# Second FFN weights kept split in DRAM, double buffers for the spectral evictions, and Winograd input sums in five steps

## The chip, the cores and the metric

The kernel runs on one core of a Trainium2 chip. The core has a matrix engine (TensorE, PE in the profile; its weight loads are listed as PEld), a vector engine (VectorE, DVE), a scalar engine (ScalarE, ACT), GpSimd (POOL) and SyncE (SP), which here only issues DMAs. Each engine works through its own queue of instructions in order and waits on semaphores that other engines or DMAs raise. Matmul operands come from SBUF, an on-chip memory of 128 partitions, and results go to PSUM banks, which VectorE and ScalarE read. DRAM is reached by DMA alone.

The metric is the device time of one execution in microseconds. The kernel before takes 1140.56 us, the median of three runs.

## The reference

The reference adds three things for a prompt `u` of 2048 rows by 576 channels: `u` itself, a state-space convolution (S4) and a feed-forward network, the last two on the layer-normalised rows.

```python
dt = exp(log_dt); A = A_re + 1j*A_im; B = B_re + 1j*B_im; C = C_re + 1j*C_im
P = exp((dt*A)[:, :, None] * l[None, None, :])          # 576 x 128 x 2048
K = einsum("dn,dnl,dn->dl", C, P, dt*B).real            # the kernel of the convolution
y = irfft2(rfft2(pad(xn.T)) * rfft2(pad(K)))[:, :2048].T + xn * Dskip
h = silu(xn @ w1)                                       # 576 -> 4608
out = u + y + h @ w2                                    # 4608 -> 576
```

All is float32.

## The kernel before, in words

**Precision.** TensorE's float32 products are made from two parts: a value `x` is split into `xh`, a rounded copy made by ScalarE, and `xl = x - xh`, made by VectorE. A product is the sum of three matmuls, `wh*xh + wh*xl + wl*xh`. So every weight tile costs a cast on ScalarE and a subtraction on VectorE before TensorE can use it.

**The FFN** sets the order of the work. Rows are processed in two halves of 1024 rows, each half in two blocks (b) of 512; the 4608 hidden channels in nine chunks (c) of four tiles (t) of 128. `up` (L278) makes one hidden tile for 512 rows: matmuls into `ph`, the SiLU and the split into `gh`, `gl` (L294 to L296). `down` (L298) multiplies four hidden tiles with the second weights for 128 rows, into two PSUM tiles `po` of 288 columns (L309), and VectorE adds each to the output accumulator `acc` (L313). The weights come with `load_w1` (L235) and `load_w2` (L260, a 288 KB DMA on SP's queue, L264) into the raw tiles `w1r` and `w2r`; `split_w1` and `split_w2` (L267) make the parts: ScalarE casts `w2h` (L273), VectorE subtracts `w2l` (L275).

**Second half, from its chunk 2 on.** `wino_ffn` (L421) takes over for seven chunks, as 14 units n of two hidden tiles. It computes the `up` matmuls of both blocks together by a Winograd form of a 2x2 block product: seven products instead of eight. `prod` (L438) is one product of six matmuls of 512 columns, `rest` (L444) adds the last 64 channels, `gate` (L447) is the SiLU and split. `prep` prepares sums of weights (L362 to L369) and their splits (`split`, L355 and L356) for the next unit. The seven products go to four accumulators: `pb`, `ps_a`, `ps_c` and the SBUF tile `f5`; the `down` steps `d[0]` to `d[3]` of the unit before lie between them. The second weights of a unit are loaded and split there by `second` as in the other chunks. The sums of the inputs S1, S2, S3, S4 are made once by `wino_x` (L548): VectorE joins the parts (L554), forms sums, and splits them again (L559, L560).

**The convolution** is worked in as side work between the FFN's steps: `side` yields at fractions of the FFN's 276 steps, and each piece is put into the program when the FFN has come that far. The tables and the kernel K are made in the first half (`kgen`). `wino_x` runs whole at 0.6215. `spectral` (L852) runs from there to 0.855, in 32 steps k: it loads two tables `m2`, `m3` on POOL's queue (L855), loads and splits a 128-row tile of both spectra on SP's queue (`load_split`), multiplies them into `pk` and `pu` (L943), forms the complex product in `ka`, `kb` (L870 to L879: ScalarE evicts `pk`, VectorE multiplies by `pu`), splits it into `yh`, `yl`, multiplies back into `pb`, and stores 288 KB `yo` to the DRAM tensor `d2` (L894, POOL). Each step is written one ahead: `front(k+1)` comes before the back part of k.

**The tail.** From 0.895 on, `tail` loads the results: `conv_load` (L946) reads a conv tile `ys` from `d2` in two DMAs (L950), with six buffers; `load_r0` (L905) reads back the first half's sums `r0` (576 KB for two row tiles). In the second half's last chunk, and for the first half's rows in `last` (L907), `add_conv` (L953) multiplies `ys` with a table (L964), and VectorE adds the result (L971); then the rows are stored. Conv tiles 8 to 15 belong to the second half, 0 to 7 to the first. The tail's loads are written behind `pins["load"]`, the last weight load issued; such a pin orders an instruction behind another on the same engine's queue.

**Who sets the order.** The program's order gives priorities; a scheduler then orders each engine's queue by when it estimates operands ready, so a queue can differ from the source's order. Blocks marked high priority (evictions, gates, `acc` adds) go ahead of other ready work.

**Buffers.** Pools give each tag a number of rotating buffers, and a tile's first write waits for the last reader of the tile that had the buffer. `w2h` and `w2l` have five each, `w2r` two, `ka` and `kb` one, all from pools that are named in the code.

Of the kernel before, what the change touches and what calls it, by code (L numbers as in the profile page):

```python
# [17 lines left out]
P = 128  # L18
# [23 lines left out]
def kernel(  # L42
# [185 lines left out]
    def ffn():  # L228
# [31 lines left out]
        def load_w2(half, c, t):  # L260

            first = half == 0 and c == 0
            r2 = (pa if first and t > 1 else wp).tile([P, D], F32, tag="w2r", name="w2r", bufs=2)
            pins["load"] = nc.sync.dma_start(r2, w2v[:, c * FT + t, :]).ins  # L264
            R2[half, c, t] = r2

        def split_w2(half, c, t):  # L267
            first = half == 0 and c == 0
            r2 = R2.pop((half, c, t))
            h2 = wp.tile([P, D], F32R, tag="w2h", name="w2h", bufs=FT + 1)  # L270
            l2 = wp.tile([P, D], F32R, tag="w2l", name="w2l", bufs=FT + 1)
            with behind(pins["xt_s"] if first else pins["gh"]):
                pins["w2h"] = nc.scalar.copy(h2, r2).ins  # L273
            with behind(pins["w1l"] if first else None):
                nc.vector.tensor_sub(l2, r2, h2)  # L275
            W2[half, c, t] = h2, l2

# [20 lines left out]
        def down(blk, jj, terms=None):  # L298
# [4 lines left out]
            for h in range(2):  # L303
                hs = slice(h * HD, (h + 1) * HD)
                po = ps2.tile([P, 512], F32, tag="ps2", name="po")
                n = 0
                for gs, ws in terms:
                    for g, w in ((0, 0), (0, 1), (1, 0)):
                        pins["pe"] = nc.tensor.matmul(po[:, :HD], gs[g][:, js], ws[w][:, hs],  # L309
                                                      start=n == 0, stop=n == 3 * len(terms) - 1).ins  # L310
                        n += 1
                with tc.high_priority():
                    nc.vector.tensor_add(acc[j][:, hs], po[:, :HD], acc[j][:, hs])  # L313
# [74 lines left out]
        for i, blk in enumerate(plain[:-1]):  # L388
# [15 lines left out]
            for step in ("u0", "d0", "d1", "d2", "d3", "u1", "u2", "u3"):  # L404
# [14 lines left out]
        yield from wino_ffn(load_w1, load_w2, split_w2, prep, WT, first, end, W2, plain[-1], down)  # L419

    def wino_ffn(load_w1, load_w2, split_w2, prep, WT, first, end, W2, before, down):  # L421

# [63 lines left out]
        for n in range(first, end):  # L486
            d = downs(n - 1)
            pb = ps2.tile([P, 512], F32, tag="ps2", name="pb2")
            f5 = wino["pool"].tile([P, 512], F32, tag="f5", name="f5", bufs=1)
            prod(pb, unit("c1", n, 0), A[0], start=True)  # L490
            with tc.high_priority():
                nc.scalar.copy(ps_a, pb)
            prod(ps_c, unit("t13", n, 0), S1, start=True)
            rest(ps_c, "c2", n, 2, x41)
            with tc.high_priority():
                nc.scalar.copy(f5, ps_c)
            yield 0
            d[0]()
            second(n, 0, "split")
            second(n + 1, 0, "load")  # L500
            yield 0
            prod(pb, unit("t24", n, 0), S2)
            with tc.high_priority():
                nc.vector.tensor_add(ps_c, pb, f5)
            d[1]()
            prep(n + 1, "c2")
            yield 0
            prod(pb, unit("t13", n, 2), S3)
            with tc.high_priority():
                nc.vector.tensor_add(f5, pb, f5)  # L510
            d[2]()
            prep(n + 1, "c1")
            prep(n + 1, "sums")
            yield 0
            d[3]()
            second(n, 1, "split")
            second(n + 1, 1, "load")
            yield 0

            def lower():  # L520
                gate(f5, 1, 2 * n + 1)
                prod(pb, unit("t24", n, 2), A22)
                gate(pb, 1, 2 * n)

            def upper():
                prod(ps_c, unit("c2", n, 0), S4)
                rest(ps_c, "c2", n, 2, d4)
                gate(ps_c, 0, 2 * n + 1)
                prod(ps_a, unit("c1", n, 2), A[1])
                rest(ps_a, "c1", n, 4, x40)  # L530
                gate(ps_a, 0, 2 * n)

            rest(pb, "c1", n, 4, x41, stop=False)
            for k, f in enumerate((lower, upper) if n % 2 == 0 else (upper, lower)):
                f()
                prep(n + 1, ("t13", "t24")[k])
                yield 0
# [10 lines left out]
    def wino_x(sx, xp):  # L548

        (ah, al, x40), (bh, bl, x41) = xts[2], xts[3]  # L550

# [11 lines left out]
        def new(name):  # L563
# [4 lines left out]
        d4 = xp.tile([P, 512], F32R, name="d4")  # L568
        x21, x22 = join(bh, bl, 0, "x21"), join(bh, bl, 2, "x22")
        nc.vector.tensor_add(x22, x21, x22)  # L570
# [13 lines left out]
        yield 0  # L584
        S3 = parts(x21, bh[:, 0:2], bl[:, 0:2])
        wino["x"] = ([(ah[:, 0:2], al[:, 0:2]), (ah[:, 2:4], al[:, 2:4])], (bh[:, 2:4], bl[:, 2:4]),
                     S1, S2, S3, S4, x40, x41, d4)
        wino["pool"] = xp

    kl = yp = pa = tail_at = None  # L590
    kf = {}
# [260 lines left out]
    def spectral():  # L852
# [5 lines left out]
        def front(k):  # L858
# [118 lines left out]
    def side():  # L977
        nonlocal s4, kl, yp, pa, tail_at
        marks = (0.1357, 0.613, 0.855)
# [136 lines left out]
```

## Time and profile before

| what | value |
|---|---|
| three runs | 1140.56, 1141.24, 1139.49 us; median 1140.56 |
| the profiled execution | 1145.05 us, its span 1143.3 us, mean granted clock 0.995 |
| TensorE busy | 1101.7 us, 96% of the span |
| VectorE busy | 981.5 us, 86% |
| ScalarE busy | 735.9 us, 64% |
| GpSimd busy | 98.5 us, 9% |
| moved by DMA | 151.26 MB, 132 GB/s on average |
| w2 casts on ScalarE (L273) | 72, 47.7 us |
| w2 subtractions on VectorE (L275) | 72, 53.5 us |
| input sums of the Winograd form | joins begin at 665.10 us |
| spectral stage | tables loaded from 685.5 us, last matmul ends at 1066.45 us |

A row of costly groups reads: line, engine, operation, output tile, its operands, shapes and count, then busy time in us and mean ns of one, then the idle time of that engine just before these instructions and what ended most of it. A row of waits reads: engine, waiting line, what ended the wait, the total in us, how often, the longest. A row of stretches gives, between two times, the busy time and count of each engine, the granted TensorE clock as a share of full speed, the mean busy share of the 16 DMA engines and the GB/s moved. A row of DMA issues gives the queue, the count, the KB of each and the median us from issue to landing. A row of the chain gives the start, the length and what ran on the path that ended last. In a timeline row the bracket is the idle time before the instruction and what released it. Matmuls overlap in the array, so the durations of single matmuls are longer than the distance between two starts.

### The profile page before, as it was taken

The page shows a single profiled execution, that of the slowest core. Times are in us where ns is not written, and L with a number is a line of the kernel's source. Part 1 is how long each engine was busy: PE and PEld are TensorE (multiplying, and loading weights), DVE is VectorE, ACT ScalarE, POOL GpSimd, SP SyncE. Part 2 cuts the span into 40 slices and gives each one's busy share as a digit, 9 for nine tenths or more (in the row PEclk, how much of TensorE's full clock was granted, in tenths as well). Part 3 has the DMA queues.
Part 4 walks back from the last instruction along what each step waited for, and adds up shares of the span by engine and source line. Part 5 has one row for each costly group of instructions (what it writes and reads, how often), then busy time and mean ns, then how long its engine had stood idle before and what let it go on. Part 6 is the DMA issues. An engine that isn't in the chain of part 4 may idle for free.

```text
span 1143.3 us, 23137 instructions
## 1 busy us (share of the span) xinstructions
PE 1101.7 (96%) x9101; PEld 989.3 (87%) x9101; DVE 981.5 (86%) x1675; ACT 735.9 (64%) x1297; POOL 98.5 (9%) x178
## 2 busy tenths in 40 slices
PE   6999999999999999999999989999999999999878
PEld 5998998988889898898899977999899888999766
DVE  6698999999999999999999688998898779888535
ACT  4665557676667677667676437787878667877310
POOL 1001000000000000000000001111111111110012
PEclk9999999999999999999999999999999999999989
DMA  9456412424232525175924136445444445442697
GB/s 272 132 161 214 126 35 80 103 91 102 90 92 60 138 74 127 47 202 187 244 75 109 44 74 181 133 138 152 135 113 144 136 133 151 149 144 90 148 236 229
DMA packets 167372, 151.26 MB, mean 132 GB/s; under 512 B 87984, under 2 KB 136128, under 8 KB 166624
## 3 DMA queue, kind: packets, MB, share of 16 engines
q1 hardware_dynamic: 150128, 112.66, 35.8%
q0 software_dynamic: 16752, 36.24, 10.1%
q8 instruction: 72, 1.18, 0.4%
q10 hardware_dynamic: 384, 0.89, 0.3%
q14 instruction: 36, 0.29, 0.1%
HBM read 103.74 MB, written 46.08 MB: 131 GB/s over the span
## 4 chain that ended last, share of the span: by engine, by line
PE 59%; DVE 18%; DMA 9%; ACT 9%; issue 3%; SPq 1%; DVEq 0%; ACTq 0%
PE po L309 26%; PE ph L286 14%; PE pb L438 3%; DMA w1r<-in_B_w_dram 3%; PE kp L818 2%; DVE acc L313 2%; PE pc L438 2%; PE z L833 1%; PE ph L287 1%; PE ph L288 1%; PE pk L943 1%; DMA dxt<-xt 1%; PE pu L943 1%; DVE w1l L356 1%; PE pb L943 1%
## 5 line engine op out<-in xcount | busy, mean ns | idle before, releaser
L309 PE MATMUL po<-w2h,gh 128*128 128x288 f32 x1152 | 339.7, 299 | 7.5 <-DVE acc L313 5.4
L309 PE MATMUL po<-w2l,gh 128*128 128x288 f32 x1152 | 339.1, 297 | 0.4 <-DVE w2l L275 0.4
L309 PE MATMUL po<-w2h,gl 128*128 128x288 f32 x1152 | 336.1, 297 | 0.6 <-DVE gl L296 0.6
L309 PEld LDWEIGHTS po<-w2h,gh 128*128 128x128 f32 x1152 | 216.1, 189 | 21.8 <-DVE acc L313 8.4
L309 PEld LDWEIGHTS po<-w2l,gh 128*128 128x128 f32 x1152 | 216.9, 189 | 8.1 <-issue 2.3
L309 PEld LDWEIGHTS po<-w2h,gl 128*128 128x128 f32 x1152 | 215.5, 189 | 3.3 <-DVE gl L296 0.9
L313 DVE TENSOR_TENSOR acc<-po,acc 128x288 f32<-128x288 f32 x296 | 129.0, 450 | 29.0 <-PE po L309 27.5
L286 PE MATMUL ph<-xh,w1h 128*128 128x512 f32 (+1 forms) x368 | 99.4, 387 | 0.9 <-ACT xh L123 0.6
L286 PE MATMUL ph<-xl,w1h 128*128 128x512 f32 (+1 forms) x368 | 98.6, 383 | 0.0
L286 PE MATMUL ph<-xh,w1l 128*128 128x512 f32 (+1 forms) x368 | 97.3, 382 | 0.0
L294 ACT ACTIVATE gf<-ph 128x512 f32<-128x512 f32 (+1 forms) x92 | 52.9, 576 | 44.3 <-PE ph L288 26.8
L273 ACT CAST w2h<-w2r 128x576 fp32r<-128x576 f32 x72 | 47.7, 674 | 47.8 <-PE po L309 32.6
L286 PEld LDWEIGHTS ph<-xl,w1h 128*128 128x128 f32 x368 | 66.5, 189 | 12.4
L286 PEld LDWEIGHTS ph<-xh,w1l 128*128 128x128 f32 x368 | 66.6, 188 | 12.1
L286 PEld LDWEIGHTS ph<-xh,w1h 128*128 128x128 f32 x368 | 65.3, 191 | 11.0 <-ACT xh L123 0.9
L777 ACT ACTIVATE c<-th,magic 128x1040 f32<-128x1040 f32 x36 | 42.0, 1167 | 43.8 <-DVE C L798 34.1
L296 DVE TENSOR_TENSOR gl<-gf,gh 128x512 fp32r<-128x512 f32 (+1 forms) x92 | 60.5, 659 | 8.8 <-ACT gh L295 8.4
L779 ACT ACTIVATE c<-th 128x1040 f32<-128x1040 f32 x36 | 38.7, 1074 | 37.9 <-DVE th L778 37.8
L295 ACT CAST gh<-gf 128x512 fp32r<-128x512 f32 (+1 forms) x92 | 55.3, 602 | 7.7 <-PE po L309 6.4
L855 POOL DMA_DIRECT2D m<-in_cm_dram x64 | 34.5, 540 | 295.8 <-PE pu L943 196.1
L157 POOL DMA_DIRECT2D d1u<-u x32 | 17.4, 542 | 451.6 <-ACT u L156 451.6
L275 DVE TENSOR_TENSOR w2l<-w2r,w2h 128x576 fp32r<-128x576 f32 x72 | 53.5, 749 | 2.0 <-ACT w2h L273 1.8
(268 smaller groups left out, 2449.6 us busy)
## 6 DMA issues: line engine op xcount, KB each, us to landing
w2r<-in_B_w_dram SPq DMA_DIRECT2D x72, 288.0 KB, 3.9
w1r<-in_B_w_dram SPq DMA_DIRECT2D x35, 512.0 KB, 3.8
d1u<-u POOLq DMA_DIRECT2D x32, 288.0 KB, 2.7
d1k<-stage SPq DMA_DIRECT2D x18, 512.0 KB, 7.2
ur<-d1u SPq DMA_DIRECT2D x32, 288.0 KB, 3.0
kr<-d1k SPq DMA_DIRECT2D x32, 288.0 KB, 2.8
d<-yo POOLq DMA_DIRECT2D x32, 288.0 KB, 2.8
ys<-d SPq DMA_DIRECT2D x32, 288.0 KB, 9.6
```

What stands on the lines that cost most here:

```text
L273: pins["w2h"] = nc.scalar.copy(h2, r2).ins
L275: nc.vector.tensor_sub(l2, r2, h2)
L286: nc.tensor.matmul(ph, w[:, kt, :], v[:, kt, a:e], start=n + kt == 0, stop=False)
L294: nc.scalar.activation(gf, ph, AF.Silu)
L295: pins["gh"] = nc.scalar.copy(gh, gf).ins
L296: pins["gl"] = nc.vector.tensor_sub(gl, gf, gh).ins
L309: pins["pe"] = nc.tensor.matmul(po[:, :HD], gs[g][:, js], ws[w][:, hs], start=n == 0, stop=n == 3 * len(terms) - 1).ins
L313: nc.vector.tensor_add(acc[j][:, hs], po[:, :HD], acc[j][:, hs])
L438: pins["pe"] = nc.tensor.matmul(dst, a[:, kt], v[:, kt], start=start and n == 0, stop=stop and n == 5, skip_group_check=True).ins
L777: nc.scalar.activation(c65, th, AF.Identity, bias=magic)
L779: nc.scalar.activation(c65, th, AF.Abs)
L855: nc.gpsimd.dma_start(m, cm23[:, k, i:i + 2])
```

## The change

It has four parts.

First, a DRAM tensor `dw2` is added, with room for the split second weights of seven chunks (28 tiles of 128 partitions by 2 by 576). In the first half, `split_w2` of the chunks 2 to 8 stores the parts there after splitting, one DMA of 576 KB a tile on SP's queue. In the second half, `second` no longer loads and splits these weights; it reads the parts back with one DMA of 576 KB a tile on POOL's queue, straight into the tile that the matmuls use. `w2h` and `w2l` become the two halves of one tile `w2`. The raw `w2r` buffers move to another pool, which exists in the first part of the kernel as well.

Second, `ka` and `kb` get two buffers each, and the split of `ka` into `yh`, `yl` is written ahead of `front(k+1)`, where it was written at the end of `front(k)`.

Third, `wino_x` yields five times, at steps 171 to 175 of 276, and its parts are spread over them: joins; S1; S2; S3 and the sum for S4; S4 and the small `d4`. The spectral stage starts at step 176 (before 0.6215 of 276, which is step 171.5), and its end mark stays at 0.855.

Fourth, the two inputs of the Winograd form change places (`xts[3], xts[2]`), and the products of a unit become named functions. The first unit has an order of its own: p1, d0, c11 and d1, d2, then p5, p6 and d3, then p7, and at the end c12 and c2x. In the later units the products keep their order; only the accumulators' roles are named anew.

```diff
+    dw2 = dram.tile([NFT - WINO_C * FT, P, 2, D], F32, name="dw2")
...
         def load_w2(half, c, t):
-            r2 = (pa if first and t > 1 else wp).tile([P, D], F32, tag="w2r", name="w2r", bufs=2)
+            r2 = (pa if first else kfp).tile([P, D], F32, tag="w2r", name="w2r", bufs=4 if first else 2)
             pins["load"] = nc.sync.dma_start(r2, w2v[:, c * FT + t, :]).ins
...
         def split_w2(half, c, t):
-            h2 = wp.tile([P, D], F32R, tag="w2h", name="w2h", bufs=FT + 1)
-            l2 = wp.tile([P, D], F32R, tag="w2l", name="w2l", bufs=FT + 1)
+            W2[half, c, t] = w = wp.tile([P, 2, D], F32R, tag="w2", name="w2", bufs=FT + 1)
+            h2, l2 = w[:, 0], w[:, 1]
...
-            W2[half, c, t] = h2, l2
+            if half == 0 and c >= WINO_C:
+                nc.sync.dma_start(dw2[(c - WINO_C) * FT + t], w.bitcast(F32))
...
-        def second(n, i, part):
-            if first <= n < end:
+        def second(n, i):
+            if n < end:
                 f = 2 * n + i
-                (load_w2 if part == "load" else split_w2)(1, f // FT, f % FT)
+                w = wp.tile([P, 2, D], F32R, tag="w2", name="w2", bufs=FT + 1)
+                pins["load"] = nc.gpsimd.dma_start(w, dw2[f - WINO_C * FT]).ins
+                W2[1, f // FT, f % FT] = w
...
-        for i in range(2):
-            second(first, i, "load")
+        second(first, 0)
...
+            def c11():
+                prod(ps_a, units["c1", n, 2], A[1])
+                rest(ps_a, "c1", n, 4, x40)
+                gate(ps_a, 1, 2 * n)
+            def c12():
+                prod(ps_c, units["c2", n, 0], S4)
+                rest(ps_c, "c2", n, 2, d4)
+                gate(ps_c, 1, 2 * n + 1)
+            def c2x():
+                gate(f5, 0, 2 * n + 1)
+                prod(pb, units["t24", n, 2], A22)
+                gate(pb, 0, 2 * n)
+            def c1x():
+                c12()
+                c11()
+            def side_w(k):
+                if k == 1:
+                    prep(n + 1, "c2")
+                elif k == 2:
+                    prep(n + 1, "c1")
+                    prep(n + 1, "sums")
+                elif k == 3:
+                    second(n, 1)
+                    second(n + 1, 0)
+            if n == first:
+                order = ((p1, 0), (c11, 1), (2,), (p5, p6, 3), (p7,))
+                ends = c12, c2x
+            else:
+                order = ((p1, p5), (0,), (p6, 1), (p7, 2), (3,))
+                ends = (c1x, c2x) if n % 2 == 0 else (c2x, c1x)
...
     def wino_x(sx, xp):
-        (ah, al, x40), (bh, bl, x41) = xts[2], xts[3]
+        (ah, al, x40), (bh, bl, x41) = xts[3], xts[2]
...
         x21, x22 = join(bh, bl, 0, "x21"), join(bh, bl, 2, "x22")
+        S1, S2, S4 = new("s1"), new("s2"), new("s4")
+        S3 = bh[:, 0:2], bl[:, 0:2]
...
+        yield 0
         nc.vector.tensor_add(x22, x21, x22)
-        S1 = parts(x22, *new("s1"))
+        parts(x22, *S1)
+        yield 0
         x11 = join(ah, al, 0, "x11")
         nc.vector.tensor_sub(x21, x11, x21)
         nc.vector.tensor_sub(x11, x22, x11)
-        S2 = parts(x11, *new("s2"))
+        parts(x11, *S2)
+        yield 0
+        parts(x21, *S3)
         x12 = join(ah, al, 2, "x12")
         nc.vector.tensor_sub(x12, x12, x11)
-        S4 = parts(x12, *new("s4"))
+        yield 0
+        parts(x12, *S4)
...
-        S3 = parts(x21, bh[:, 0:2], bl[:, 0:2])
...
-            ka = kl.tile([P, D], F32, tag="ka", name="ka")
-            kb = kl.tile([P, D], F32, tag="kb", name="kb")
+            ka = kl.tile([P, D], F32, tag="ka", name="ka", bufs=2)
+            kb = kl.tile([P, D], F32, tag="kb", name="kb", bufs=2)
...
-            return m3, split_of(ka, "y", 1)
+            return m3, ka
...
-            m3, ys = nxt
+            m3, y = nxt
+            ys = split_of(y, "y", 1)
             if k < 31:
                 nxt = front(k + 1)
...
-            for _ in wino_x(sx, xp):
-                yield 0.6215
+            for k, _ in enumerate(wino_x(sx, xp)):
+                yield (171 + k) / 276
         with tc.tile_pool(name="kl", bufs=1) as kl:
             for at in spectral():
-                yield 0.6215 + (at - 1) * (marks[2] - 0.6215)
+                yield 176 / 276 + (at - 1) * (marks[2] - 176 / 276)
```

More of the change, by code (lines that the diff above doesn't have):

```diff
@@ L418, in ffn, with wino_ffn @@
                         prep(first, early[step])
-        yield from wino_ffn(load_w1, load_w2, split_w2, prep, WT, first, end, W2, plain[-1], down)
-    def wino_ffn(load_w1, load_w2, split_w2, prep, WT, first, end, W2, before, down):
+        yield from wino_ffn(load_w1, prep, WT, first, end, W2, plain[-1], down)
+    def wino_ffn(load_w1, prep, WT, first, end, W2, before, down):
         ps_a = ps1.tile([P, 512], F32, tag="ps1", name="pa")
@@ L489, in wino_ffn @@
             f5 = wino["pool"].tile([P, 512], F32, tag="f5", name="f5", bufs=1)
[L490 to L526, printed above, removed]
-                rest(ps_c, "c2", n, 2, d4)
[L528 to L531, printed above, removed]
+            units = {k: unit(*k) for k in (("c1", n, 0), ("c1", n, 2), ("t13", n, 0), ("t13", n, 2),
+                                           ("t24", n, 0), ("t24", n, 2), ("c2", n, 0))}
@@ new lines, in p1, with p5, p6 @@
+            def p1():
+                prod(pb, units["c1", n, 0], A[0], start=True)
+                with tc.high_priority():
+                    nc.scalar.copy(ps_a, pb)
+            def p5():
+                prod(ps_c, units["t13", n, 0], S1, start=True)
+                rest(ps_c, "c2", n, 2, x41)
+                with tc.high_priority():
+                    nc.scalar.copy(f5, ps_c)
+            def p6():
+                prod(pb, units["t24", n, 0], S2)
+                with tc.high_priority():
+                    nc.vector.tensor_add(ps_c, pb, f5)
@@ new lines, in p7 @@
+            def p7():
+                prod(pb, units["t13", n, 2], S3)
+                with tc.high_priority():
+                    nc.vector.tensor_add(f5, pb, f5)
+            def c11():
[4 more added lines that the diff above has]
+                prod(ps_c, units["c2", n, 0], S4)
+                rest(ps_c, "c2", n, 2, d4)
+                gate(ps_c, 1, 2 * n + 1)
[3 more added lines that the diff above has]
+                gate(pb, 0, 2 * n)
@@ L533, in wino_ffn @@
+            for steps in order:
+                for f in steps:
+                    if callable(f):
+                        f()
+                    else:
+                        d[f]()
+                        side_w(f)
+                yield 0
             rest(pb, "c1", n, 4, x41, stop=False)
-            for k, f in enumerate((lower, upper) if n % 2 == 0 else (upper, lower)):
+            for k, f in enumerate(ends):
                 f()
@@ L977, in side @@
     def side():
-        nonlocal s4, kl, yp, pa, tail_at
+        nonlocal s4, kl, yp, pa, kfp, tail_at
         marks = (0.1357, 0.613, 0.855)
```

11 lines of the change are left out of this document (6 added, 5 removed).

## The prediction

> **What bounds the kernel now.** I read the page first, then busy time by stretches, the waits, the chain of the last 83 us and the timeline of single engines. The page says which engine to watch:
>
> ```profile
> span 1143.3 us, 23137 instructions
> PE 1101.7 (96%) x9101; PEld 989.3 (87%) x9101; DVE 981.5 (86%) x1675; ACT 735.9 (64%) x1297; POOL 98.5 (9%) x178
> ...
> L273 ACT CAST w2h<-w2r 128x576 fp32r<-128x576 f32 x72 | 47.7, 674 | 47.8 <-PE po L309 32.6
> ...
> L275 DVE TENSOR_TENSOR w2l<-w2r,w2h 128x576 fp32r<-128x576 f32 x72 | 53.5, 749 | 2.0 <-ACT w2h L273 1.8
> ```
>
> PE is busy 96% of the span and the number of matmuls does not change. What can be won is PE's idle time and its time at a reduced clock. The stretches show where these lie:
>
> ```profile
> core 0: us, PE busy (x) PEld busy (x) DVE busy (x) ACT busy (x) POOL busy (x), PEclk, DMA share, GB/s
> ...
> 665.00:682.00 17.00, 13.05 (x82) 11.20 (x81) 16.83 (x22) 5.39 (x8) 0.86 (x1) 1.00 0.20 58
> 682.00:698.40 16.40, 13.68 (x77) 11.68 (x75) 12.41 (x21) 10.04 (x18) 2.63 (x5) 1.00 0.55 158
> 698.40:701.80 3.40, 3.33 (x14) 3.33 (x15) 3.25 (x6) 3.30 (x8) 0.12 (x1) 0.51 0.18 39
> 716.00:800.00 84.00, 84.00 (x529) 77.79 (x528) 73.87 (x142) 64.97 (x138) 11.37 (x21) 1.00 0.48 140
> 800.00:900.00 100.00, 98.46 (x619) 90.34 (x618) 84.32 (x161) 77.53 (x165) 14.62 (x27) 1.00 0.46 134
> 900.00:1000.00 100.00, 98.02 (x602) 88.46 (x601) 85.94 (x165) 76.39 (x163) 13.01 (x24) 1.00 0.46 140
> 1000.00:1060.00 60.00, 59.84 (x380) 55.16 (x379) 50.89 (x99) 44.39 (x95) 7.57 (x14) 1.00 0.38 113
> 1078.00:1097.60 19.60, 11.55 (x99) 7.85 (x98) 5.71 (x13) 0.00 (x0) 3.91 (x8) 1.00 1.08 245
> 1097.60:1104.50 6.90, 6.02 (x30) 3.94 (x31) 0.92 (x2) 0.67 (x1) 0.00 (x0) 0.51 1.07 283
> 1104.50:1143.30 38.80, 33.12 (x343) 26.61 (x342) 19.64 (x46) 4.61 (x8) 6.79 (x14) 0.98 0.76 216
> ```
>
> Three stretches differ. At 665 to 702 PE idles while DVE is full (16.83 of 17.00): the start of the Winograd units. From 716 to 1060 PE idles only 3.7 of 344 us. From 1078 the DMA engines are full (share 1.08) and PE waits. The waits that end there, and some that the change touches:
>
> ```profile
> PE py L964 <- DMA ys<-d: 8.9, 3, 3.1
> PE pu L943 <- ACT kb L873: 2.6, 1, 2.6
> PE pb L438 <- ACT s2h L559: 1.3, 1, 1.3
> ACT ka L870 <- DVE yl L930: 13.2, 21, 1.4
> ACT w2h L273 <- DMA w2r<-in_B_w_dram: 15.1, 9, 3.2
> ```
>
> The chain of the last 83 us has the tail's stream, and two rows that give PE's pace: 3.18/24 = 0.133 us per 288-column matmul, 1.39/6 = 0.232 per 512-column one. With these I turn positions in the built order of both kernels into PE time.
>
> ```profile
> 1061.11 3.18 PE po L309 x24
> ...
> 1066.17 0.28 PE pb L943 x2
> ...
> 1075.70 11.35 DMA r<-dr
> 1087.06 11.29 DMA ys<-d
> ...
> 1105.32 1.39 PE pc L438 x6
> ```
>
> The last spectral matmul (pb) ends at 1066.45. The second r0 tile lands at 1087.05 (20.6 later) and conv tile c4 at 1098.35 (31.9 later); between them c6, c3, c7, c4 landed: 2.8 us a tile.
>
> **The change, part by part.**
>
> *The removed splits.* 28 casts at 674 ns take 18.9 us off ACT, 28 subtractions at 749 ns 21.0 us off DVE, all in the second half. Together with the second ka/kb buffers and the y split placed ahead of the next front (ACT's 13.2 us of waits on yl, not PE's), this can return to PE at most its idle 3.7 us of 716 to 1060. I take 1.5, a little under half, because DVE there is at 84 to 88%: the waits are chance collisions, not a shortage. Bounds 0 and 3.
>
> *The Winograd start.* The timeline, DVE and then PE:
>
> ```profile
> 665.10 4.63 DVE L554 TENSOR_TENSOR x<-xh,xl 128x1024 f32<-128x1024 f32 x4 [0.45 <-DMA d1k<-stage]
> ...
> 670.25 0.75 DVE L275 TENSOR_TENSOR w2l<-w2r,w2h 128x576 fp32r<-128x576 f32 x1
> 670.92 0.55 DVE L356 TENSOR_TENSOR w1l<-w1r,w1h 128x384 fp32r<-128x384 f32 x1
> 671.39 0.45 DVE L313 TENSOR_TENSOR acc<-po,acc 128x288 f32<-128x288 f32 x1
> ...
> 683.63 1.21 DVE L560 TENSOR_TENSOR s4l<-x,s4h 128x1024 fp32r<-128x1024 f32 x1
> ...
> 685.21 0.70 DVE L504 TENSOR_TENSOR pc<-pb,f 128x512 f32<-128x512 f32 x1
> ```
>
> ```profile
> 671.89 0.40 PE L309 MATMUL po<-w2h,gh 128*128 128x288 f32 x1 [2.66 <-DVE acc L313]
> ```
>
> Four joins and a subtraction run on DVE in one block, an acc add behind them, and PE waits 2.66 us for the PSUM bank. In the built order of the changed kernel the block is still whole (the scheduler does not spread the joins over the five steps), but w2l and w1l no longer stand between it and the acc add; they took 670.25 to 671.39, 1.1 us: the wait becomes 1.5. S1's low part keeps its place on DVE while PE comes earlier: 1.2 new. S2 is needed 12 matmuls (1.6 us) later, but PE is 1.2 earlier: the 1.3 becomes 0.9. S2's last and S3's first products become neighbours on PE (before, 12 down matmuls, 1.6 us, lay between), and pc<-pb (0.70) stands behind s4l on DVE: 1.6 new. At the start of the spectral stage PE reaches its first pk about 6 us later against the loads, so the 2.60 wait for kb goes and with it, I assume, the 3.4 us at 0.51 (half of it, 1.7). Four w2 reads are now ahead of the second matrices on POOL; with 6 us of slack I give them nothing, and 2.6 if the slack is gone. Before: 2.66 + 1.26 + 2.60 + 1.7 = 8.2. After: 1.5 + 1.2 + 0.9 + 1.6 = 5.2. Gain 3.0; bounds 0 (each new wait as long as an old one) and 5.5 (the S1 and S3 waits do not appear).
>
> *The reads of w2 on POOL.* 28 DMAs of 576 KB enter POOL's queue among the m loads and the d stores. A unit's first tile can be issued when a down matmul frees a buffer, and has 5.9 to 8.3 us of PE work to its first use; the second 31 to 38; the m loads keep 11 to 16. No row has this transfer. The nearest:
>
> ```profile
> w2r<-in_B_w_dram SPq DMA_DIRECT2D x72, 288.0 KB, 3.9
> ...
> d<-yo POOLq DMA_DIRECT2D x32, 288.0 KB, 2.8
> ys<-d SPq DMA_DIRECT2D x32, 288.0 KB, 9.6
> m<-in_cm_dram POOLq DMA_DIRECT2D x64, 128.0 KB, 2.4
> ...
> r<-dr SPq DMA_DIRECT2D x4, 576.0 KB, 8.1
> ...
> xl<-dxt POOLq DMA_DIRECT2D x2, 1024.0 KB, 5.3
> ```
>
> On POOL 128 KB take 2.4 and 1024 KB 5.3; 576 KB by the line between them 3.9. The upper bound is 8.1, of r<-dr in the full tail. At 3.9 nothing waits; I put 0.5 for the tightest units. By the Trainium skill, page "DMA: Bandwidth & Descriptors", section "Anatomy of one DMA — SWDGE (gpsimd) path" (2.0 us plus bytes at 436 GB/s), it would be an estimated 3.4, and the sum 0.5 lower. The issue itself is short:
>
> ```profile
> L855 POOL DMA_DIRECT2D m<-in_cm_dram x64: 537/537/599, 685.5 to 1050.7; - x64
> ```
>
> 64 issues differ by 62 ns at most although DVE is 84 to 88% busy. The Trainium skill, page "SBUF — State Buffer", section "SBUF: two separate sides", warns that DMAs issued from GpSimd wait for their descriptors while VectorE runs a two-port operation (3100 instead of 620 ns); it counts tensor_tensor, the form of the DVE rows shown, as without that mode, and this row shows no such stall. By the warning each read would land 2.5 later, 6.4: an estimate.
>
> *The stores in the first half.* 28 stores of 576 KB join SP's queue; each waits for a w2l, and the reload of w2r behind it waited for that already. ACT waits 15.1 us there for w2r, but PE is seldom behind it: a loss of 0.5, bounds 0 and 2.
>
> *The tail.* The spectral stage starts at step 176 instead of 171.5 and ends at the same one; in the built order its last pb stands at matmul 7078 of 7679 instead of 7256, 29 us of PE work earlier. That does not free the conv tiles as such: they are read back through the same queue.
>
> ```profile
> 1076.52 26.34 SPq L950 DMA_DIRECT2D ys<-d  x16
> ```
>
> After the last pb, c4 was needed after 22.1 us of PE work and c5 after 30.3; now 27.1 and 34.3. But the pin of the tail's loads no longer holds SP back (the last load is now POOL's, and the pin binds one engine only), so the last w1 tile (512 KB and two of 64) comes behind c7 in SP's queue, ahead of c4 and c5, and w2 reads run beside them. At 283 GB/s (the row 1097.60:1104.50) a 576 KB tile takes 2.1 us. c4 then lands at 31.9 + 2.0 (w2 pair, partly in the idle time before the stream) + 2.3 (w1) = 36.2; c5, three tiles of 2.8 behind it and so before at 40.3, at 44.6: PE has waited 9.1 and then 10.3 us in all, with 1.7 for a half clock 12.0. Before: 8.9 and half of 6.9 at 0.51 = 12.3. I call that gain 0. Upper bound: both w2 tiles land in time (c5 at 42.6, wait 8.3, no half clock): gain 4.0. Lower bound: the chain's 2.8 a tile, with the two last w2 reads ahead of c5: 40.3 + 2.8 + 3.1 + 5.6 = 51.8, wait 17.5, half clock 3.4: loss 8.6.
>
> **Sum**: -3.0 - 1.5 + 0.5 + 0.5 + 0 = -3.5 us. The profiled execution took 1145.05 (span 1143.3), 0.4% over the median 1140.56 of the runs. Its span becomes 1139.8; taken off the median, 1137.0.
>
> **The rivals.**
> Slower, by the tail's stream: the last w1 load and w2 reads queue among the conv tiles at 2.8 us each. For it: DMA share 1.08 there. Against: it needs the late w2 reads to win against SP's queue. The loss of 8.6 gives 1137.0 + 8.6 = 1145.6; it turns the sign once c5 lands over 48.4 us after the last pb (wait 14.1 + 1.7 = 12.3 + 3.5).
> Slower, by late w2 reads: at 8.1 us against about 7.1 of cover each of 13 units waits 1.0: 1137.0 - 0.5 + 13 = 1149.5. It decides from about 6 on. For it: only r<-dr, with full engines; the middle has a DMA share of 0.46. The SBUF page's warning is this rival's other way in.
> No change: the new waits at S1 and S3 eat the start's gain, and the removed splits were hidden: 1140.6. For it: 3.7 us of idle time in 344.
> Much faster: 5.5 at the start, 3 in the middle, 4.0 in the tail, less 0.5: 1128.6. For it: the spectral stage ends 29 us earlier. Against: the w1 load in the stream.
>
> **How the numbers follow.** A measurement of this kernel tells about 0.2% (2.3 us) from no change: faster is below 1138.3, slower above 1142.8. Forecast 0.50, own range 1133 to 1140 (0.42 faster, 0.07 same, 0.01 slower); much faster 0.10; no change 0.18 (0.03, 0.11, 0.04); tail 0.15 and w2 reads 0.07, slower. Together 0.55, 0.18, 0.27. The range 1129 to 1146 leaves out the late reads and the outer halves of the tail's and the much faster case, about 0.19.
>
> **What would show it.** In the profile after: the wait of PE for acc near 1.5 us where the joins end, new waits in front of pc<-s1l and of S3's products, none for kb, and no stretch at half clock about 700. No wait of PE or PEld for w2<-dw2, and landings near 4 us. PE idle under 3 us over the middle. In the tail three to five waits for ys<-d of 9 to 12 us in all. The forecast is wrong if c5 lands over 48 us after the last pb, if w2<-dw2 takes over 6, or if the joins delay more than one acc add.

## The result, and the profile after

The changed kernel takes 1137.41 us (median of 20 runs, 1134.69 to 1142.80), the kernel before on the same chip 1142.38 us (20 runs, 1136.91 to 1145.22). The ratio, of the means, is 0.9964, with a 95% interval of 0.9952 to 0.9977: 4.1 us faster, where 3.5 were forecast. (The two medians lie 5.0 apart.)

The profiled execution took 1137.18 us, its span is 1135.4. The page of the changed kernel, with the rows of its new DMAs:

```profile
span 1135.4 us, 23108 instructions
PE 1098.5 (97%) x9101; PEld 990.3 (87%) x9101; DVE 962.0 (85%) x1647; ACT 721.6 (64%) x1269; POOL 113.3 (10%) x206
...
dw<-w SPq DMA_DIRECT2D x28, 576.0 KB, 4.7
w<-dw POOLq DMA_DIRECT2D x28, 576.0 KB, 5.6
```

VectorE lost 19.5 us of work and ScalarE 14.3; the span fell by 7.9. Where it fell is seen when both executions are cut at the same events: the start of the Winograd units (660 to 716), then up to the end of the last spectral matmul (1066.4 before, 1030.3 after), then the tail. Busy time by stretches of the kernel before:

```profile
0.00:660.00 660.00, 643.47 (x6118) 580.17 (x6119) 603.10 (x961) 425.69 (x651) 34.87 (x59) 1.00 0.43 122
660.00:716.00 56.00, 49.26 (x273) 43.07 (x272) 47.76 (x76) 32.66 (x60) 5.23 (x9) 0.97 0.49 130
716.00:1066.40 350.40, 346.72 (x2165) 317.79 (x2164) 299.98 (x572) 267.32 (x568) 47.12 (x87) 1.00 0.44 132
1066.40:1143.30 76.90, 62.29 (x550) 48.31 (x548) 30.70 (x68) 10.19 (x19) 11.24 (x23) 0.95 0.86 224
```

and of the changed kernel:

```profile
0.00:660.00 660.00, 644.39 (x6116) 581.85 (x6117) 602.82 (x961) 426.77 (x651) 35.37 (x60) 1.00 0.50 147
660.00:716.00 56.00, 50.93 (x279) 44.35 (x278) 44.26 (x71) 31.56 (x57) 6.25 (x11) 0.97 0.51 141
716.00:1030.30 314.30, 312.86 (x1984) 290.04 (x1983) 271.61 (x524) 244.16 (x528) 57.71 (x107) 1.00 0.54 162
1030.30:1135.40 105.10, 90.33 (x728) 74.01 (x726) 43.29 (x92) 19.15 (x35) 14.01 (x28) 0.97 0.73 195
```

Length less PE's busy time is PE's idle time. It went from 16.5 to 15.6 us in the first part, from 6.7 to 5.1 at the start of the units, from 3.7 to 1.4 in the middle, and stayed in the tail (14.6, 14.8). That is 4.7 us of the 7.9 by which the two spans differ; the execution before that was profiled lay 2.7 us over its median. The clock explains none of the rest: its mean was 0.995 before and 0.994 after. In the tail it took 3.8 us (0.05 of 76.9) before and 3.2 (0.03 of 105.1) after, at the start of the units 1.7 in both, and in the changed kernel 1.7 more in the first half, which the row of 660 us rounds away:

```profile
570.00:580.00 10.00, 8.21 (x52) 7.42 (x51) 6.50 (x9) 4.49 (x9) 0.00 (x0) 0.83 0.76 236
```

The rest is in delays that the rows count as busy. A 288-column matmul is listed with 0.30 us, but the next one starts 0.133 us after it, so a delay of up to 0.17 us leaves no gap. An estimate of all lost time, idle, slow clock and short delays together, comes from the distances between the starts of matmuls, each less the median distance of its kind (shape and output tile) in the traces of all kernels here. Lost us in the four stretches, each kernel cut at its own last spectral matmul (a value below zero is faster than the median):

| kernel | first part | start of the units | middle | tail |
|---|---|---|---|---|
| before | 32.5 | 9.7 | 7.8 | 26.0 |
| changed | 33.0 | 8.0 | 2.4 | 24.5 |
| `start_only` (this and the next: below) | 32.6 | 8.1 | 5.6 | 36.2 |
| `dw2_only_b` | 29.0 | 9.3 | 6.3 | 24.9 |
| `one_buf` | 34.7 | 7.7 | 8.5 | 25.5 |
| `old_start_b` | 30.7 | 10.5 | 4.4 | 25.1 |
| `old_order` | 33.6 | 10.6 | 0.2 | 21.3 |
| `reads_sp` | 31.3 | 8.0 | -0.6 | 23.7 |

Between before and changed these add up to 8.1 us, and 5.4 of them are in the middle, where idle time shows 2.2. One trace a kernel is not exact: three kernels with the same program up to there (changed, `tail940`, `tail932`) lost 2.4, 2.2 and 4.5 us in the middle.

PE's waits in the changed kernel:

```profile
PE py L998 <- DMA ys<-d: 8.2, 5, 3.7
PE po L311 <- DVE acc L315: 2.9, 2, 2.4
...
PE po L311 <- ACT gh L456: 1.8, 1, 1.8
...
PE py L998 <- issue: 1.1, 1, 1.1
PE pk L977 <- DVE kb L911: 0.8, 2, 0.5
PE pb L440 <- DVE pc L510: 0.8, 1, 0.8
...
PE po L311 <- DMA w<-dw: 0.3, 1, 0.3
PE pu L977 <- ACT kb L906: 0.2, 1, 0.2
```

### The profile page after: what moved, and what is told of

Same layout as the page of the kernel before. It is cut to its first block, busy times and chain, and to the rows that moved or that the text cites. A ratio compares the mean times of both kernels' runs of the same rounds, so it can differ in the third digit from the quotient of the medians.

```text
span 1135.4 us, 23108 instructions
## 1 busy us (share of the span) xinstructions
PE 1098.5 (97%) x9101; PEld 990.3 (87%) x9101; DVE 962.0 (85%) x1647; ACT 721.6 (64%) x1269; POOL 113.3 (10%) x206
## 3 DMA queue, kind: packets, MB, share of 16 engines
q0 software_dynamic: 20784, 52.76, 14.8%
## 4 chain that ended last, share of the span: by engine, by line
PE 71%; DVE 11%; DMA 9%; ACT 4%; issue 4%; SPq 1%; POOL 0%; DVEq 0%; ACTq 0%; POOLq 0%
PE po L311 30%; PE ph L288 16%; PE pb L440 5%; DMA w1r<-in_B_w_dram 3%; PE pc L440 3%; PE kp L851 2%; PE pk L977 2%; PE pu L977 2%; DMA ys<-d 2%; PE pb L977 2%; DVE acc L315 1%; PE ph L289 1%; PE ph L290 1%; PE pa L440 1%; DMA w2r<-in_B_w_dram 1%
## 5 line engine op out<-in xcount | busy, mean ns | idle before, releaser
L311 PE MATMUL po<-w,gh 128*128 128x288 f32 x2304 | 478.8, 298 | 8.8 <-DVE acc L315 2.9
L311 PEld LDWEIGHTS po<-w,gh 128*128 128x128 f32 x2304 | 379.3, 189 | 26.4 <-issue 4.2
L311 PE MATMUL po<-w,gl 128*128 128x288 f32 x1152 | 337.8, 298 | 0.6 <-DVE gl L298 0.6
L311 PEld LDWEIGHTS po<-w,gl 128*128 128x128 f32 x1152 | 216.9, 189 | 3.4 <-DVE gl L298 0.9
L357 ACT CAST w1h<-w1r 128x512 fp32r<-128x512 f32 (+2 forms) x56 | 34.6, 622 | 40.1 <-DMA w1r<-in_B_w_dram 30.9
L888 POOL DMA_DIRECT2D m<-in_cm_dram x64 | 34.4, 539 | 230.0 <-PE pu L977 178.8
L830 DVE TENSOR_TENSOR S<-th,C 128x1024 f32<-128x1024 f32 x36 | 44.0, 1221 | 10.0 <-ACT th L813 9.9
L358 DVE TENSOR_TENSOR w1l<-w1r,w1h 128x512 fp32r<-128x512 f32 (+2 forms) x56 | 38.4, 687 | 10.8 <-ACT w1h L357 10.6
L457 DVE TENSOR_TENSOR gl<-gf,gh 128x512 fp32r<-128x512 f32 x56 | 38.0, 688 | 9.2 <-ACT gh L456 8.8
```

The lines of the kernel that those rows point to most:

```text
L311: pins["pe"] = nc.tensor.matmul(po[:, :HD], gs[g][:, js], ws[:, w, hs], start=n == 0, stop=n == 3 * len(terms) - 1).ins
L358: nc.vector.tensor_sub(l[:, :k], src, h[:, :k])
L830: nc.vector.tensor_mul(ov3, t[:, :, 0:64].rearrange("n d (x y) -> n d x y", y=32), mv3)
```

## The experiments

Twelve kernels were run, each beside the kernel before on the same chip; the ratios are to that. The changed kernel was not run again beside them, so that a comparison with its 0.9964 goes over two chips.

**Taking the parts away.** Three parts can be undone: the weights in DRAM, the second buffers with the late y split, and the new start.

`one_buf` takes the second away from the changed kernel:

```diff
-            ka = kl.tile([P, D], F32, tag="ka", name="ka", bufs=2)
-            kb = kl.tile([P, D], F32, tag="kb", name="kb", bufs=2)
+            ka = kl.tile([P, D], F32, tag="ka", name="ka")
+            kb = kl.tile([P, D], F32, tag="kb", name="kb")
...
-            return m3, ka
+            return m3, split_of(ka, "y", 1)
```

> The changed kernel with one buffer each for ka and kb, and the y split back at the end of front: split weights in DRAM and the new start stay. In its built order the last spectral matmul stands at 7258 (before 7257, changed 7079). My prediction's terms (start -3.0, splits and buffers together -1.5 of which half may go, w2 traffic +1.0) give about -2.8 us, a ratio of 0.9975 to the kernel before. The theory from the trace of after (the gain came from 800 to 1000 and needs both the fewer splits and the second buffers) gives half of it or less: -1.6 at the start and about -0.5 in the middle, 0.998 to 0.999. If the buffers do nothing, 0.9964 as the whole change.

Measured: 1.0005 (0.9992 to 1.0019). Without the second buffers the whole gain is gone, although 28 casts and 28 subtractions are still saved. Its busy time by the same stretches, from 716 on:

```profile
716.00:1067.50 351.50, 347.19 (x2174) 318.65 (x2173) 288.57 (x557) 259.65 (x558) 60.45 (x112) 1.00 0.50 150
1067.50:1144.00 76.50, 63.26 (x549) 49.60 (x547) 29.38 (x65) 7.70 (x15) 11.80 (x24) 0.92 0.91 243
```

PE is idle 4.3 us in the middle (3.7 before, 1.4 in the changed kernel), and the tail loses 13.2 us idle and 0.08 of 76.5 by the clock, 19.4 in all (18.5 before, 17.9 in the changed kernel).

The two halves of that part, each alone in the changed kernel: `buf_only` has two buffers, with the y split back at the end of `front`; `late_split` has one buffer, with the split ahead of the next front.

> The changed kernel with the y split back at the end of front, but two buffers each for ka and kb. Last spectral matmul at 7093. If the buffers give the 4.7 us that lie between one_buf and the changed kernel, 0.9964 to 0.9975; if the place of the split does, 1.000.

> The changed kernel with one buffer each for ka and kb, but the y split ahead of the next front. Last spectral matmul at 7258, as in one_buf. If the buffers give the gain, 1.000 to 1.001 as one_buf; if the place of the split does, 0.9964 to 0.9975.

Measured: 0.9974 (0.9949 to 0.9999) and 0.9984 (0.9973 to 0.9995). Neither expectation holds alone: both halves are below 1 and neither interval separates from the other; the two together give more than either centre.

`start_only` takes both other parts away: weights loaded and split as before, one buffer.

> The new Winograd start alone: weights loaded and split in the second half as before, one buffer for ka and kb. Last spectral matmul at 7335, 78 later than before. By the prediction -3.0 us, 0.9974. By the trace of after -1.6 at the start, and the later end of the spectral stage takes cover from the tail's reads: 0.9985 to 1.001.

Measured: 1.0079 (1.0065 to 1.0092), far above both. Its stretches:

```profile
660.00:716.00 56.00, 50.80 (x283) 44.56 (x283) 48.28 (x78) 33.57 (x61) 4.69 (x8) 0.97 0.44 120
716.00:1075.70 359.70, 357.03 (x2234) 328.16 (x2233) 303.41 (x579) 270.03 (x574) 47.65 (x88) 1.00 0.44 131
1075.70:1149.10 73.40, 57.12 (x472) 42.31 (x470) 25.35 (x59) 6.06 (x11) 11.22 (x23) 0.82 0.86 230
```

At the start PE idles 5.2 us instead of 6.7, as in the changed kernel, and in the middle 2.7 instead of 3.7. The loss is in the tail: 16.3 us idle and 0.18 of 73.4 by the clock, 29.5 against 18.5. The spectral stage ends 78 matmuls later (7335 for 7257, 10 us of PE work at 0.133), and the tail pays 11.

`old_start` and `dw2_only` undo the start in the changed kernel, the second with one buffer as well. In both, S3 is formed a step earlier than in the kernel before, over parts that the last plain `up` products still read: those products use changed inputs, and wait for them. So these two compute something else than the reference, and no price is taken from them. The two with a b at the end form S3 one step later, as the kernel before does (its `wino_x` has one break, ahead of S3). `old_start_b` has `wino_x` of the kernel before, and:

```diff
-            if n == first:
-                order = ((p1, 0), (c11, 1), (2,), (p5, p6, 3), (p7,))
-                ends = c12, c2x
-            else:
-                order = ((p1, p5), (0,), (p6, 1), (p7, 2), (3,))
-                ends = (c1x, c2x) if n % 2 == 0 else (c2x, c1x)
+            order = ((p1, p5), (0,), (p6, 1), (p7, 2), (3,))
+            ends = (c2x, c1x) if n % 2 == 0 else (c1x, c2x)
...
-            for k, _ in enumerate(wino_x(sx, xp)):
-                yield (171 + k) / 276
+            for _ in wino_x(sx, xp):
+                yield 0.6215
```

The diff also puts back the order of the two ends of every later unit (`c1x`, `c2x`): the change had exchanged them with the inputs, so that the blocks kept their order and the products did not.

> The changed kernel with the old Winograd start: input sums made whole at 0.6215, spectral stage from 0.6215, the two inputs in their old places, the first unit in the order of the others; split weights in DRAM and second buffers stay. Last spectral matmul at 6957. By the prediction's terms the start's 3.0 us are lost and -0.5 is left: 0.9996. By the trace of after the start gave 1.6 and the middle over 5: it stays at 0.9965 to 0.998, and the tail's waits, with the spectral stage ending 120 matmuls earlier still, do not grow.

> The second weights split in the first half, kept in DRAM and read back, alone: old start, one buffer for ka and kb. Last spectral matmul at 7138. By the prediction w2 reads and stores cost 1.0 and the missing splits return about 0.8: 1.0002. By the trace of after the fewer splits are a part of the middle's gain: -1 to -3 us, 0.9975 to 0.999. By the rival of late w2 reads it is slower than before.

> As old_start, with S3 formed one step after the other sums, where the kernel before forms it, so that no plain product waits for it. Last spectral matmul at 7073 (changed 7079). By the prediction's terms -0.5 us is left of the change, 0.9996. By the trace of after the start is worth 1.6 us of the 4.1: 0.9978. If the start is worth nothing, 0.9964.

> As dw2_only, with S3 formed one step after the other sums. Last spectral matmul at 7248 (before 7257). By the prediction's terms (w2 traffic +1.0, missing splits about -0.8) 1.0002. If the splits taken off ScalarE and VectorE give what the middle gained, 0.997. Late w2 reads would show as over 1.003.

Measured: `old_start` 0.9971 (0.9958 to 0.9984), `dw2_only` 1.0088 (1.0066 to 1.0111), `old_start_b` 1.0023 (1.0006 to 1.0040), `dw2_only_b` 1.0005 (0.9994 to 1.0017). The last says what the prediction said (1.0002): the weights in DRAM, alone, neither give nor take. The runs of `old_start_b` spread from 1139.93 to 1151.02 us and the profiled one was its fastest, so its trace does not show its loss; the profiled run of `dw2_only_b` (1138.78, median 1143.75) was its fastest too. `old_order` puts back the inputs and the first unit's order, but keeps the five steps and the later spectral start:

> The changed kernel with the two inputs of the Winograd form in their old places and the first unit in the order of the others; input sums in five steps and the spectral stage from step 176 stay. old_start_b, which undoes both, gave 1.0023. If the first unit's order carries the start's gain, 1.000 to 1.003; if the five steps and the later spectral start do, 0.9964 to 0.998. By the prediction, which gave the gain to work that no longer stands ahead of the acc add and to PE reaching the spectral stage later, about 0.998.

Measured: 0.9946 (0.9927 to 0.9964), no slower than the whole change. The first unit's order does show where it acts, at the start of the units:

```profile
660.00:716.00 56.00, 49.72 (x273) 43.91 (x272) 42.97 (x69) 29.62 (x55) 6.80 (x13) 0.94 0.52 143
```

```profile
PE pk L973 <- ACT kh L959: 1.7, 1, 1.7
```

PE idles 6.3 us there and loses 3.4 by the clock, where the changed kernel has 5.1 and 1.7; it waits for the first operands of the spectral stage, as in `old_start_b` (1.3). But the middle and the tail lose less (0.2 and 21.3 us for 2.4 and 24.5), so the whole gets no slower. That leaves the five steps and the spectral start at 176 as what separates it from `old_start_b`; but the built orders of the two differ on every engine, and which of these differences costs the 9 us between them was not settled.

**Where the reads are issued.**

```diff
-                pins["load"] = nc.gpsimd.dma_start(w, dw2[f - WINO_C * FT]).ins
+                pins["load"] = nc.sync.dma_start(w.bitcast(F32), dw2[f - WINO_C * FT]).ins
```

> The changed kernel with the w2 reads on SP's queue instead of POOL's. In the trace of after PE waited 0.3 us in all for these reads, and the second matrices' median landing rose from 2.4 to 3.0 us. If the reads are hidden wherever they are issued, 0.9955 to 0.998; if sharing POOL's queue with the matrices and the stores costs something, below 0.995; if SP's queue, which holds the spectra's reads, is the worse place, above 0.998.

Measured: 0.9921 (0.9895 to 0.9946), 1132.17 us, the fastest of all. Its stretches:

```profile
716.00:1028.60 312.60, 312.60 (x1991) 290.90 (x1991) 271.28 (x521) 245.22 (x529) 47.74 (x89) 1.00 0.53 163
1028.60:1129.10 100.50, 87.23 (x708) 72.25 (x707) 42.85 (x91) 17.82 (x34) 11.21 (x23) 0.95 0.76 204
```

PE is not idle at all in the middle, and the tail is as before (13.3 idle, 5.0 by the clock). The tile itself lands no sooner. For the reads on POOL (changed kernel) and then on SP, the views of that line and the row of each queue's waits give:

```profile
L467 POOL DMA_DIRECT2D w<-dw x28: 537/540/594, 630.2 to 1103.6; - x28
...
DMA to landing us min/median/max: 3.9/5.6/10.5
```

```profile
POOL w L467 <- PE po L311: 58.2, 10, 17.4
```

```profile
L467 SPq DMA_DIRECT2D w<-dw x28: 319/376/1192, 634.5 to 1098.7; - x28
...
DMA to landing us min/median/max: 3.5/5.8/10.7
```

```profile
SPq L467 <- PE po L311: 66.8, 18, 19.4
```

Both queues stand in front of these reads until a down matmul frees the buffer: POOL for 58.2 us in ten waits, SP for 66.8 in eighteen. So a queue that is held up is not by itself what the reads cost on POOL. What stands behind them differs (matrices and stores on POOL, the spectra and the first weights on SP; in the middle the stores' median landing went from 4.1 to 3.2 us), and so does the built order of every engine, with the last spectral matmul at 7098 instead of 7079. Which of these gives the 4.9 us between the two kernels stays open.

**The tail's cover.** The built orders show the first conv products right behind the last spectral matmul in both kernels (13 us of PE work after it in the changed one, 10 before). The spectral stage ends earlier, but the conv products moved with it. Written later, they leave time for the reads:

```diff
-        tail_at = (0.895, 0.0055, 0.919, 0.0052)
+        tail_at = (0.895, 0.0055, 0.940, 0.0052)
```

> The changed kernel with the first half's conv products written later (0.940 instead of 0.919). In the built order the last spectral matmul stays at 7079, and the first six conv tiles are used 24, 28, 30, 35, 42 and 47 us of PE work after it instead of 13, 15, 16, 19, 24 and 30. The theory: in the changed kernel the spectral stage ends 29 us of PE work earlier, but the conv products moved with it, so the reads got no more cover; with cover the waits for conv tiles (8.2 us and 1.1 of issue in the trace of after) and the clock lost behind them go, and the ratio to the kernel before falls from 0.9964 to 0.988 to 0.991. If the tail is bound by the DMA stream whatever the order (the prediction's tail, gain 0), the waits only move to later tiles and it stays at 0.995 to 0.998.

> As tail940 with 0.932: the first six conv tiles are used 13, 18, 29, 29, 34 and 37 us of PE work after the last spectral matmul. By the theory of cover the waits for the first four go and about half for the fifth and sixth stay (c5 landed about 45 us after): 0.990 to 0.994, between the changed kernel and tail940. If the stream binds, 0.995 to 0.998.

Measured: 0.9934 (0.9912 to 0.9955) and 0.9942 (0.9918 to 0.9966). Both centres are lower than the change's, by about half of what was expected of `tail940` and less than expected of `tail932`; both intervals still touch the changed kernel's. The only wait of PE in the tail of `tail940`, and what stood before it on ScalarE and VectorE:

```profile
PE po L311 <- DVE acc L315: 6.7, 1, 6.7
```

```profile
1060.95 1.14 ACT L357 CAST w1h<-w1r 128x384 fp32r<-128x384 f32 x2 [17.91 <-DMA w1r<-in_B_w_dram]
```

```profile
1061.49 1.45 DVE L358 TENSOR_TENSOR w1l<-w1r,w1h 128x384 fp32r<-128x384 f32 x2 [9.66 <-ACT w1h L357]
1062.86 0.42 DVE L368 TENSOR_TENSOR w1r<-w1r 128x256 f32<-128x256 f32 x1
1063.19 0.45 DVE L315 TENSOR_TENSOR acc<-po,acc 128x288 f32<-128x288 f32 x1
```

The 8.2 us of waits for conv tiles are gone, and one of 6.7 has come: the last w1 tile, behind the conv tiles in SP's queue, is late, its splits stand ahead of an `acc` add on VectorE, and PE waits for the PSUM bank. It is the last w1 load of the prediction's first rival, in a later place.

## Why the prediction was right, and where its steps were not

**The sum.** Forecast 1137.0 us, measured 1137.41; -3.5 us forecast, -4.1 measured. The closeness of the two times is in part luck: the forecast was taken off 1140.56, the median of three runs, and the kernel before took 1142.38 in twenty. The terms, forecast and as the table of lost time shows them: the start -3.0, measured -1.7; the middle -1.5, measured -5.4; the tail 0, measured -1.5; the stores +0.5, measured +0.5 (the whole first part); the w2 reads +0.5, measured 0.3 us of waits, which are part of the middle. By the two traces that is -8.1, by the twenty runs -4.1, as the profiled execution before was a slow one. The sum came out because the start was put too high and the middle, beyond its bound of 3, too low.

**The start.** The 1.1 us that w2l and w1l took ahead of the acc add were saved, as the DVE timeline of the changed kernel shows:

```profile
666.37 4.63 DVE L581 TENSOR_TENSOR x<-xh,xl 128x1024 f32<-128x1024 f32 x4 [1.35 <-DMA d1k<-stage]
670.92 0.69 DVE L616 TENSOR_TENSOR e<-x,x 128x512 f32<-128x512 f32 x1
671.52 0.82 DVE L315 TENSOR_TENSOR acc<-po,acc 128x288 f32<-128x288 f32 x2
```

but the joins began 1.27 us later (666.37 for 665.10), since they wait for a store of the convolution's kernel, and PE waited 2.42 instead of the 1.5 forecast. I had seen that release in the row of before and not asked whether the store would land at the same time. The new waits for S1 (1.2) and S2 (0.9) did not come, that at S3 was 0.8 and not 1.6, and one that I had not listed came: 1.8 for a gate of the first unit (L456). The wait for kb went, as forecast, but the half clock was not saved. It moved:

```profile
665.00:682.00 17.00, 14.58 (x85) 13.37 (x84) 15.59 (x22) 6.96 (x10) 0.86 (x1) 0.90 0.20 47
...
698.00:702.00 4.00, 4.00 (x26) 3.64 (x25) 3.79 (x9) 3.94 (x10) 0.00 (x0) 1.00 0.27 79
```

0.10 of 17 us is the same 1.7, now behind the wait of 2.42. The kernel before had waited 2.66 in that stretch at a clock of 1.00. The Trainium skill, page "TensorE: Matmul & The Clock Gate", section "Part 1: The HAM clock gate (the "warmup" mystery)", lets the clock fall after an idle window of about 3.4 us. Here stretches with waits of 1.79 (at 576 us, below), 2.42 and 2.60 had it, and one with 2.66 had not, nor one of 1.5 at the place of the 1.79 in `reads_sp`. Whether a wait of this length costs the clock can't be read from its length.

**The splits and the buffers.** The prediction had both in one term, and took PE's idle 3.7 us as the most that could come back. That is the step that failed: 7.8 us were lost in the middle, and 5.4 of them came back. The splits alone did not bring them. Where only the weights in DRAM were added, the loss in the middle went from 7.8 to 6.3 us (before, `dw2_only_b`) and from 5.6 to 8.5 (`start_only`, `one_buf`), no gain clear of what traces of one program differ by, though 40 us of work had left ScalarE and VectorE: the prediction's "chance collisions, not a shortage". With the second buffers and the late split it fell from 8.5 to 2.4 (`one_buf`, changed), and the ratio from 1.0005 to 0.9964, 4.7 us. But that price holds beside the new start only, for the parts do not add up:

| ratio to the kernel before | old start | new start |
|---|---|---|
| neither | 1 | 1.0079 |
| weights in DRAM | 1.0005 | 1.0005 |
| weights in DRAM, second buffers with the late split | 1.0023 | 0.9964 |

Beside the old start the buffers gave nothing. Beside the new start the weights in DRAM gave 8.5 us, nearly all in the tail (25.5 us lost for 36.2). Every one of these kernels also has a built order of its own, and why the start decides over the rest is not shown. The two second buffers take twice 2304 bytes a partition, as much as the two raw w2 tiles that the change moves out of the pool that lives to the end. The second buffers without the weights in DRAM were not tried.

**The stores.** The first part lost 0.5 us more, as forecast; but the changed kernel, `tail940` and `tail932`, which have the same first half, lost 33.0, 34.4 and 35.1 us in it, so that the size is not settled. The place can be seen. In the first half ScalarE waits 5.4 us for one raw tile (1.9 there before), with a gate behind it, and PE waits for the gate; the half clock at 576 us follows:

```profile
574.36 0.67 ACT L274 CAST w<-w2r 128x576 fp32r<-128x576 f32 x1 [5.44 <-DMA w2r<-in_B_w_dram]
```

```profile
576.23 0.97 PE L311 MATMUL po<-w,gh 128*128 128x288 f32 x4 [1.79 <-ACT gh L297]
```

In every kernel with the stores but `dw2_only_b` PE waits there, 1.2 us or more; in the two without them, before and `start_only`, it does not. (The raw tiles' other pool comes with the stores; the two were not separated.) Other waits of the first part became shorter, so that PE's idle time there fell by 0.9 us.

**The w2 reads.** The landing was mis-sized: 5.6 us at the median and 10.5 at most, where 3.9 and 8.1 were taken (the Trainium skill's formula, named in the prediction, gave 3.4). It cost PE 0.3 us, so the cover of 5.9 to 8.3 was long enough for nearly all of them. On POOL the issues took 537 to 594 ns beside a busy VectorE, and on SP the reads landed no sooner: the stall by descriptors that the Trainium skill warns of (page "SBUF — State Buffer", section "SBUF: two separate sides") did not occur here. What POOL's queue cost beside these waits is open (`reads_sp`).

**The tail.** Here the landings held to a few tenths, while the waits for them were 8.2 us for 10.3. The last spectral matmul started at 1030.3; PE's timeline and SP's:

```profile
1058.09 1.38 PE L998 MATMUL py<-ys,s 64*32 64x288 f32 x16 [3.67 <-DMA ys<-d]
1066.52 0.84 PE L998 MATMUL py<-ys,s 64*32 64x288 f32 x16 [1.85 <-DMA ys<-d]
1075.43 0.69 PE L998 MATMUL py<-ys,s 64*32 64x288 f32 x8 [1.68 <-DMA ys<-d]
```

```profile
1040.39 8.12 SPq L984 DMA_DIRECT2D ys<-d  x6
1049.31 0.46 SPq L243 DMA_DIRECT2D w1r<-in_B_w_dram  x1
1052.61 0.81 SPq L244 DMA_DIRECT2D w1r<-in_B_w_dram  x1
1053.77 0.49 SPq L245 DMA_DIRECT2D w1r<-in_B_w_dram  x1
1055.10 13.57 SPq L984 DMA_DIRECT2D ys<-d  x10
```

These waits end 36 and 45 us after it for c4 and c5 (forecast 36.2 and 44.6), and the last w1 load lies among the conv tiles. The reason given for that was wrong: with the pin left on the last SP load the built order is the same on every engine. The w1 load, issued at 1049.3 us (1043.8 before), lies among them because the tail's loads follow the spectral stage and now begin at 1034.2 (1070.6 before). And an earlier end of that stage is worth little while the conv products follow it: 78 matmuls later cost 11 us (`start_only`), 178 earlier gave 0.5, or 1.5 by the table.

**The rivals.** None decided. The tail's stream had the place of the rival, at the lower of its two prices; no late reads; of the "much faster" case the middle came, and not the start (1.7 for 5.5) nor the tail (1.5 for 4.0). Of the three signs of being wrong, one is near: two `acc` adds stood behind the joins (the row with x2), though PE waited long for one only.

## What to carry to other kernels

Work taken off an engine that is not the bound can be worth nothing: here 40 us less of splits left the middle as it was. Parts of a change need not add up: the second buffers gave 4.7 us beside the new start and nothing beside the old, so a part is priced only beside those that it comes with. Idle time on a profile is no bound for what can be won, since delays shorter than the overlap of two matmuls count as busy; distances between starts show them. When a stage is made to end earlier, look where the reader of its result is placed; if it follows at the same distance, no transfer gained cover.

## What the runs showed of the hardware

The 28 reads of 576 KB landed in 5.6 us at the median from POOL and 5.8 from SP, of issues of 540 and 376 ns. The tail of `start_only` ran at a granted clock of 0.82 over 73.4 us, with waits for conv tiles of 3.0 us at most; waits in a row cost there 13.2 us by the clock, nearly as much as the 16.3 of idle time.
